# Adaptive-LayerNorm attention block: the early transfers as 128-row pieces, the first V tiles by column chunk, and group 1's V tiles in step

## The chip, the core and the metric

The kernel runs on one core of a Trainium2 chip. The core has five engines that the text calls by short names: PE (TensorE, matrix products, with PEld for its weight loads), DVE (VectorE), ACT (ScalarE), POOL (GpSimd) and SP (SyncE, which here only issues transfers). Sixteen DMA engines move data between HBM and the on-chip memory. The metric is the device time of one execution in microseconds, lower is better.

## The reference, cut to what matters

The input x has 2048 rows of 448 numbers. A vector c gives six modulation vectors of 448, three for the attention half (sa, ca, ga) and three for the other half.

```python
mod = (silu(c) @ w_mod).reshape(1, 6, 1, 448)          # c: 448, w_mod: 448 x 2688
sa, ca, ga, sb, cb, gb = (mod[:, i] for i in range(6))
h = layernorm(x) * (1 + ca) + sa
q, k, v = split(h @ wqkv)                              # wqkv: 448 x 1344, 16 heads of 28
x = x + ga * (softmax(q @ k.T * 28 ** -0.5) @ v) @ wo
h = layernorm(x) * (1 + cb) + sb
x = x + gb * gmlp(h, w_in, w_sp, b_sp, w_out)
```

Everything is float32. The change lies in the first part: mod, h, and the products of h with wqkv.

## The kernel before, in words

**Operands in two parts.** The operands of these products have the format fp32r. Each is written as the sum of a rounded part ("hi", an ACT activation that copies float32 into the format) and the rest ("lo", a subtraction, `sub`, L83). The 448 input columns are cut in chunks c = 0, 1, 2 of 128 and c = 3 of 64. hT[g] holds, for group g of 512 rows of x, slots 0 to 2 (hi of the chunks), 3 to 5 (lo) and 6 (hi and lo of the 64-row chunk, one above the other). A weight tile has the same slots and a slot 7. One product is the sum over the 11 pairs of slots in STEPS (L27 to L29), so 11 matmuls into one PSUM bank.

**Units of work.** A V tile (`v_mm`, L301) is 11 matmuls for 128 rows of x, and `v_copy` (L308, ACT) takes it out of PSUM. A q/k unit (`qk_unit`, L317) is 11 matmuls with 512 columns for one block m of 128 outputs and one group; ACT rounds the result (qh, L336) and DVE subtracts (ql). `ln_next` (L537) makes hT of a group: PE transposes the normalised rows (xn) into four banks (L117), ACT makes `hfull` (L124) and hi (L131) of each chunk, DVE the lo part, and in between the statistics of the group after it; POOL computes the scale (L107, L108), DVE the normalised rows (`ln_norm`, L286), and ACT copies their last 64 columns (L298).

**Order.** The order of each engine is the order in which the program text issues its instructions (manual schedule); nothing is moved. What one engine must wait for on another is set by the tiles: who writes a buffer waits for the last reader of what lay there before.

**PSUM.** There are eight banks. Seven form a ring: `bank` (L167) takes the first of the list `banks` and puts it at the end, so a new tile waits for the readers of the tile seven requests ago. The eighth, ps_o (L144), is asked for by name.

```python
    def bank(name):
        k = mode[0](name) if mode[0] else banks[0]
        banks.remove(k)
        banks.append(k)
        return ring.tile([128, 512], F32, name=name, tag=f"b{k}")
```

**The head.** x of group 0 comes in three pieces, the first two from ACT's queue (L181). The modulation weights of the pair (sa, ca) come in four pieces of 112 rows (`load_mod`, L176), V's weights in three pieces of 128 rows and two of 64, the same 64 rows put in both halves (`load_z`, L86), then x of group 1 and the "a" columns (0 to 511) of the q/k weights. silu(c) is made on ACT and DVE. The product with w_mod is a weighted sum on DVE over the four pieces (`acc`, L241) and then, chunk by chunk, `mod_last` (L407) and a dot with ones on PE (`mod_dot`, L420), which puts the sum of the partitions in one PSUM column; `mod_cols` (L423) takes it out. Then `h_hi` (L440), `h_full` (L431, on DVE) and `h_lo` (L445) make hT[0]. Between these steps PE runs matmuls whose result nobody reads (`pe_fill`, L228). The four V tiles of group 0 run in step (`v_step`, L474): the pair of slots is the outer loop, the tile the inner.

**After the head.** `qk_unit((0, 3), 0)` with both units in step (L530), `ln_next(1)` (L550), x of group 3, units 1 and 2 of group 0, the "b" columns of the q/k weights (L555). For group 1 the loop at L557 does V tiles 4 and 5, `ln_next(2)`, V tiles 6 and 7, then units 0 and 3, with one piece of the next modulation pair on DVE (`mod_acc`, L234) after each of the last four. Groups 2 and 3 follow the same way, then attention and the second half, to which the edits of `wo_load`, `win_first` and `win_load` belong.

Of the kernel before, what the change touches and what calls it, by code (L numbers as in the profile page):

```python
# [33 lines left out]
def tile_adaln_mha_gmlp(ctx, tc, x, wqkv, wo, w_in, w_spT, b_sp, w_out, cT, w_mod, out):  # L34
# [21 lines left out]
    silu = const.tile([112, 4], F32, name="silu")  # L56
# [6 lines left out]
    heapF = dpool.tile([128, 4 * 896], F32R, name="heapF", tag="heapF")  # L63
# [17 lines left out]
    wqk = Halves(4, hview(heapD[2], 0, 4, 896), hview(heapF, 0, 4, 896))  # L81

    def sub(eng, dst, a, hi):  # L83
        eng.tensor_tensor(out=dst, in0=a, in1=hi.bitcast(F32), op=ALU.subtract)  # L84

    def load_z(eng, dst, src):  # L86
        eng.dma_start(dst[0:64], src)
        eng.dma_start(dst[64:128], src)
# [71 lines left out]
    ones_r = e2.tile([112, 128], F32R, name="ones_r")  # L160
# [12 lines left out]
    def load_mod(pair, eng):  # L173
        for k in range(4):
            wms[pair, k] = e1.tile([112, 2, D], F32, name="wm", tag=("wm", "wm", "raw")[pair], bufs=4)
            eng.dma_start(wms[pair, k], w_mod[:, pair, k])  # L176

    def load_x(g, eng):
        xg = e1.tile([128, 4, D], F32, name="xg")
        for t0, t1 in ((0, 1), (1, 2), (2, 4)) if g == 0 else ((0, 4),):  # L180
            (act if t1 - t0 == 1 else eng).dma_start(xg[:, t0:t1, :], x[g, :, t0:t1])  # L181
        for t in range(4):
            xts[4 * g + t] = xg[:, t, :]
# [4 lines left out]
    def load_w(kind, i, eng):  # L188
        c0, n, tag = PARTS[kind]
        raw = e1.tile([128, 2 * D], F32, name="raw", tag=tag, bufs=4)[:, :n]  # L190
        if i < 3:
            eng.dma_start(raw, wqkv[i * 128 : (i + 1) * 128, c0 : c0 + n])
        else:
            load_z(eng, raw, wqkv[384:448, c0 : c0 + n])
        raws[kind, i] = raw
# [11 lines left out]
    cc_t = e1.tile([112, 4], F32, name="cc_t", bufs=1)  # L207
    sp.dma_start(cc_t, cT)
    load_x(0, sp)
    load_mod(0, sp)  # L210
    for i in (0, 2, 1, 3):
# [3 lines left out]
    pool.memset(wqk[64:128, 7, 0:896].bitcast(F32), 0.0)  # L215
# [3 lines left out]
    ec = e1.tile([112, 4], F32, name="ec", bufs=1)  # L219
    act.activation(ec, cc_t, AF.Exp, scale=-1.0)  # L220
    dve.tensor_scalar(out=ec, in0=ec, scalar1=1.0, scalar2=None, op0=ALU.add)
    dve.reciprocal(ec, ec)
    dve.tensor_tensor(out=silu, in0=cc_t, in1=ec, op=ALU.mult)

    pcs = {c: bank("pc") for c in (0, 2)}
# [8 lines left out]
    def mod_acc(pair, k):  # L234
        if k == 0:
            accs[pair] = e2.tile([112, 2, D], F32, name="acc")
        wm, acc = wms.pop((pair, k)), accs[pair]
        if k == 0:
            dve.tensor_scalar(out=acc, in0=wm, scalar1=silu[:, 0:1], scalar2=None, op0=ALU.mult)
        else:  # L240
            dve.scalar_tensor_tensor(out=acc, in0=wm, scalar=silu[:, k : k + 1], in1=acc, op0=ALU.mult, op1=ALU.add)  # L241

    def mod_split(pair, eng, pool_l, tag_l, bufs_l):
# [3 lines left out]
        for part in range(2):  # L247
            h = stage.tile([128, 512], F32R, name="acc_h", tag="qf")[0:112, :D]
            l = pool_l.tile([112, D], F32R, name="acc_l", tag=tag_l, bufs=bufs_l)
# [50 lines left out]

    def v_mm(kt):  # L301
# [12 lines left out]

    HI_FIRST = [p for p in STEPS if p[1] in (0, 1, 2, 6)] + [p for p in STEPS if p[1] in (3, 4, 5, 7)]
# [33 lines left out]
    def wv_hi(i):  # L349
        h = wv[:, i if i < 3 else 6, :]  # L350
        if i == 2:
            pool.tensor_copy(h, raws["v", i])
        else:
            act.activation(h, raws["v", i], AF.Copy)
# [8 lines left out]


    tps, fs = {}, {}
# [3 lines left out]
    def tp_first(t):  # L369
        for c in range(4):  # L370
            pe.transpose(tps[c][:, t * 128 : (t + 1) * 128], xn1[0][t][:, c * 128 : (c + 1) * 128], ident)

    x0, x3 = xts[0], xts[3]
    pe_fill(14, x0)
    ln_stat(0, (0, 1))
    ln_rs(0, 0, 2)
    ln_stat(0, (2, 3))
    ln_rs(0, 2, 4)
    accs[0] = e2.tile([112, 2, D], F32, name="acc")
    act.activation(accs[0], wms.pop((0, 0)), AF.Copy, scale=silu[:, 0:1])  # L380
    ln_norm(0, (0, 1))
    mod_acc(0, 1)
    tp_first(0)
    tp_first(1)
    ln_norm(0, (2, 3))
    mod_acc(0, 2)
    pe_fill(5, x3)
    tp_first(2)
    tp_first(3)
    pe_fill(2, x3)  # L390

    acc0 = [stage.tile([128, 512], F32, name="acc0", tag="qh")[0:112] for _ in range(2)]
    wm3 = wms.pop((0, 3))

    def mod_last(c):
        for part in (1, 0):
            if c < 3:
                o = acc0[part][:, c * 128 : (c + 1) * 128]  # L400
                a, w = (v[:, part, c * 128 : (c + 1) * 128] for v in (accs[0], wm3))
            else:
                o = acc0[part][:, 384:512].rearrange("p (r n) -> p r n", n=64)
                a, w = (
                    v[:, part, 384:D].rearrange("p (r n) -> p r n", r=1).broadcast_to([112, 2, 64]) for v in (accs[0], wm3)
                )
            dve.scalar_tensor_tensor(out=o, in0=w, scalar=silu[:, 3:4], in1=a, op0=ALU.mult, op1=ALU.add)  # L407

    def mod_dot(c, which):
        if c == 1:  # L410
            pcs[c] = ps_o.tile([128, 512], F32, name="pc", tag="o")
        if c == 3:
            pcs[c] = pcs[1][:, 2:4]
# [1073 lines left out]
```

## Time and profile before

| what | value |
|---|---|
| three executions | 1396.37, 1396.84, 1398.13 us (median 1396.84) |
| the profiled execution: its span, first to last instruction | 1394.0 us |
| what lies around the span, against the median | 2.84 us |
| PE busy | 1386.8 us of it |
| DVE, ACT, POOL busy | 1027.5, 776.5, 285.5 us |

The profile is one execution, and times in it count from its first instruction. The span is that execution's own time as the profile has it; no other time was taken of it. A row of the timeline gives the start, the time that the engine was busy, the engine, the line of the code, the operation, what it writes and reads, and how many instructions were merged in the row (x4); square brackets tell how long the engine stood idle before and who ended that. Rows of groups give busy time and the mean duration in ns, then the idle time before them. A row by stretch gives for each engine the busy time and the number of instructions, then the granted clock of PE (1.00 is full), the busy share of the DMA engines and the GB/s that they moved. Matmuls overlap, so the duration of one is longer than its distance to the next. Where two lines share a helper, the tile names tell them apart: L84 is every `sub`.

### The profile page before, as it was taken

How to read it: one execution, taken by the hardware profiler on the slowest of the kernel's cores; microseconds unless marked ns; L12 is line 12 of the kernel's file. 1: busy time of each engine (PE TensorE's matmuls, PEld its weight loads, DVE VectorE, ACT ScalarE, POOL GpSimd, SP SyncE). 2: the span in 40 equal slices, each digit the busy share in tenths (PEclk: the TensorE clock that was granted, in tenths of full speed). 3: DMA queues.
4: the chain of work that ended last, by engine and by line, in shares of the span. 5: the costliest groups of instructions: out<-in, count | busy, mean ns of one | idle time of the engine just before them, and what ended most of it. 6: DMA issues, size and time to landing. Idle time of an engine off the chain costs nothing.

```text
span 1394.0 us, 20327 instructions
## 1 busy us (share of the span) xinstructions
PE 1386.8 (99%) x7180; PEld 988.9 (71%) x7180; DVE 1027.5 (74%) x1741; ACT 776.5 (56%) x1490; POOL 285.5 (20%) x306
## 2 busy tenths in 40 slices
PE   8999999999999999999999999999999999999999
PEld 8888655555555555555555555988998888888888
DVE  7798888888888888888888851750366655668574
ACT  4623677777766667777777779363234544434211
POOL 2234213221224143323200021000142330000000
PEclk9999999999999999999999999999999999999999
DMA  8564644565465556554323002434103333445453
GB/s 265 150 178 177 196 109 151 172 177 154 149 178 167 162 159 189 165 161 150 111 68 76 21 18 73 161 123 140 46 4 110 113 109 112 143 137 163 142 174 110
DMA packets 99377, 187.01 MB, mean 134 GB/s; under 512 B 17736, under 2 KB 29130, under 8 KB 96730
## 3 DMA queue, kind: packets, MB, share of 16 engines
q1 hardware_dynamic: 96558, 181.42, 42.6%
q10 hardware_dynamic: 2718, 4.30, 0.9%
q8 instruction: 56, 0.92, 0.3%
q14 instruction: 45, 0.37, 0.1%
HBM read 130.42 MB, written 50.46 MB: 130 GB/s over the span
## 4 chain that ended last, share of the span: by engine, by line
PE 99%; DMA 0%; DVE 0%; ACT 0%; ACTq 0%; issue 0%
PE st_ps L666 19%; PE o_ps L681 17%; PE mt L634 17%; PE acc L1250 7%; PE acc L1252 7%; PE acc L1251 7%; PE z_ps L1176 5%; PE pq L323 5%; PE z_ps L1062 5%; PE wo_ps L928 3%; PE pv L305 2%; PE y_ps L1357 2%; PE y_ps L1358 2%; PE y_ps L1356 2%; PE tp L117 1%; PE pv L477 1%
## 5 line engine op out<-in xcount | busy, mean ns | idle before, releaser
L639 DVE TENSOR_REDUCE pm<-mt 128x1 f32<-128x512 f32 x1024 | 631.1, 682 | 85.6 <-PE mt L634 85.5
L670 ACT ACTIVATE P<-st_ps 128x512 f32<-128x512 f32 x1024 | 514.5, 628 | 200.8 <-PE st_ps L666 200.7
L666 PE MATMUL st_ps<-qst,kst 128*128 128x512 f32 x1024 | 404.1, 406 | 0.0
L634 PE MATMUL mt<-kst,qst 128*128 128x512 f32 x1024 | 401.7, 392 | 0.0
L666 PEld LDWEIGHTS st_ps<-qst,kst 128*128 128x128 f32 x1024 | 191.2, 187 | 141.2 <-issue 93.1
L681 PE MATMUL o_ps<-P,V 128*32 128x512 f32 x2048 | 247.1, 598 | 0.0
L634 PEld LDWEIGHTS mt<-kst,qst 128*128 128x128 f32 x1024 | 192.4, 188 | 31.8
L791 POOL TENSOR_TENSOR ws_raw<-ws_raw 128x512 f32<-128x512 f32 x80 | 103.2, 1290 | 293.8 <-DMA ws_raw<-in_w_spT_dram 290.9
L1138 ACT ACTIVATE wsp_h<-raw_sp 128x512 fp32r<-128x512 f32 x112 | 70.0, 630 | 153.6 <-PE acc L1252 102.9
L84 DVE TENSOR_TENSOR wsp_l<-raw_sp,wsp_h 128x512 fp32r<-128x512 f32 x112 | 80.7, 730 | 83.1 <-ACT wsp_h L1138 82.3
L681 PEld LDWEIGHTS o_ps<-P,V 128*32 128x32 f32 x2048 | 54.7, 109 | 122.0 <-issue 114.0
L1250 PE MATMUL acc<-wsp_h,heapA 128*128 128x512 f32 x224 | 87.3, 390 | 0.0
L1251 PE MATMUL acc<-wsp_l,heapA 128*128 128x512 f32 x224 | 87.2, 389 | 0.0
L1252 PE MATMUL acc<-wsp_h,heapA 128*128 128x512 f32 x224 | 87.2, 389 | 0.0
L1251 PE MATMUL acc<-wsp_l,heapB 128*128 128x512 f32 x174 | 67.7, 389 | 0.0
L1252 PE MATMUL acc<-wsp_h,heapB 128*128 128x512 f32 x174 | 67.7, 389 | 0.0
L1250 PE MATMUL acc<-wsp_h,heapB 128*128 128x512 f32 x174 | 67.7, 389 | 0.0
L323 PE MATMUL pq<-heapD,heapD 128*128 128x512 f32 x196 | 61.8, 390 | 0.0
L1180 DVE BATCH_NORM_STATS2 stz<-z 128x6 f32<-128x448 f32 x32 | 19.9, 625 | 50.4 <-ACT z L1179 30.1
L1250 PEld LDWEIGHTS acc<-wsp_h,heapA 128*128 128x128 f32 x224 | 42.0, 188 | 8.9 <-DVE cD L1256 0.3
L1252 PEld LDWEIGHTS acc<-wsp_h,heapA 128*128 128x128 f32 x224 | 42.0, 188 | 8.8
L1251 PEld LDWEIGHTS acc<-wsp_l,heapA 128*128 128x128 f32 x224 | 42.0, 188 | 8.6
(222 smaller groups left out, 1597.0 us busy)
## 6 DMA issues: line engine op xcount, KB each, us to landing
ws_raw<-in_w_spT_dram SPq DMA_DIRECT2D x160, 256.0 KB
ws_scr<-ws_raw SPq DMA_DIRECT2D x80, 256.0 KB
raw_sp<-ws_scr SPq DMA_DIRECT2D x80, 256.0 KB
kst<-qk_scr SPq DMA_DIRECT2D x45, 224.0 KB
qst<-qk_scr SPq DMA_DIRECT2D x45, 224.0 KB
raw_sp<-in_w_spT_dram SPq DMA_DIRECT2D x32, 256.0 KB
qk_scr<-qh SPq DMA_DIRECT2D x28, 256.0 KB
qk_scr<-ql SPq DMA_DIRECT2D x28, 256.0 KB
```

Source lines behind the costliest of these rows:

```text
L84: eng.tensor_tensor(out=dst, in0=a, in1=hi.bitcast(F32), op=ALU.subtract)
L323: pe.matmul(pq, wqk[:, b, m * 128 : (m + 1) * 128], hT[g][:, a, :], start=j == 0, stop=j == NST - 1)
L634: pe.matmul(mt, qst[h % 3][:, t * 128 : (t + 1) * 128], kst[h % 3][:, kb * 512 : (kb + 1) * 512], start=True, stop=True)
L639: dve.tensor_reduce(out=pms[h][:, t, kb : kb + 1], in_=mt, axis=AX.X, op=ALU.max)
L666: pe.matmul(st, kst[h % 3][:, kt * 128 : (kt + 1) * 128], qst[h % 3][:, qb * 512 : (qb + 1) * 512], start=True, stop=True)
L670: act.activation(p, st, AF.Exp, scale=SCALE)
L681: pe.matmul(otile[h][32 * qb : 32 * qb + 32, :], V[:, kt, h, :], ptiles.pop((u, qb)), start=kt == 0, stop=kt == NT - 1)
L791: pool.tensor_tensor(out=a, in0=a, in1=b, op=SUMS[i // 16][2])
L1138: act.activation(hi, raw, AF.Copy)
L1250: pe.matmul(acc[i], zh, hi, start=st == 0, stop=False)
L1251: pe.matmul(acc[i], zh, lo, start=False, stop=False)
L1252: pe.matmul(acc[i], zl, hi, start=False, stop=st == 7)
```

## The change

**Transfers.** The host repeats the last 64 rows of wqkv, wo and w_in, so that the fourth piece of each weight is one transfer of 128 rows; `load_z` is gone. w_mod of the first pair is laid out by column chunk: piece c has 128 rows, each with the chunk's columns for three blocks of 128 inputs and both vectors, and the last 64 inputs of the one vector above those of the other. The pairs 1 and 2 keep their four steps, now with 128 rows, the last one folded in the same way. silu becomes a 128x5 tile, whose last two columns are zero in one half. The first pair lies in the buffer of the upper q/k weight slots (heapF), which is taken for them only after the head. All of x goes through SP, c through ACT; chunks and V weights alternate in the order 0, 2, 3, 1; the "a" loads are issued after the head's work instead of in its midst.

**Head.** Chunk 0 of the modulation is eight matmuls on PE (`mod_direct`); the other chunks start with a product on ACT (`acc_first`), go on with four weighted sums on DVE (`acc_rest`) and end with the dot with ones. PE fills once, 10 pairs of instructions, instead of 27 in five places. `h_full` goes from DVE to ACT, the lo part of chunk 0 from POOL to DVE, the hi part of V's weights 2 from POOL to ACT. The V steps run chunk by chunk.

**Behind the head.** Unit 1 of group 0 goes ahead of `ln_next(1)`. Group 1's four V tiles run in step, in three banks of the ring and ps_o, with `ln_next(2)` called after the ninth step; their copies and the first two `mod_acc` follow the loop.

The core of the diff (edits of sizes from 112 to 128, the repeated rows and removed definitions are left out):

```diff
+    wm0 = dpool.tile([128, 4 * 896], F32, name="wm0", tag="heapF")
...
+    def load_mod0(c, eng):
+        n = 128 if c < 3 else 64
+        v = wm0[:, c * 896 : c * 896 + 7 * n]
+        eng.dma_start(v, w_mod0[c * 896 * 128 : (c * 896 + 7 * n) * 128].rearrange("(r n) -> r n", r=128))
+        wms[0, c] = v[:, 0 : 6 * n].rearrange("r (k p n) -> r k p n", k=3, p=2), v[:, 6 * n :]
...
-        if i < 3:
-            eng.dma_start(raw, wqkv[i * 128 : (i + 1) * 128, c0 : c0 + n])
-        else:
-            load_z(eng, raw, wqkv[384:448, c0 : c0 + n])
+        eng.dma_start(raw, wqkv[i * 128 : (i + 1) * 128, c0 : c0 + n])
...
-    sp.dma_start(cc_t, cT)
+    act.dma_start(cc_t, cT)
     load_x(0, sp)
-    load_mod(0, sp)
-    for i in (0, 2, 1, 3):
+    for i in (0, 2, 3, 1):
+        load_mod0(i, sp)
         load_w("v", i, sp)
     load_x(1, sp)
...
+    def half_rows(wm, outs):
+        for part, o in enumerate(outs):
+            dve.scalar_tensor_tensor(out=o, in0=wm, scalar=silu[:, 3 + part : 4 + part], in1=o, op0=ALU.mult, op1=ALU.add)
...
+    CHUNKS = [(0, 0), (0, 3), (3, 0), (2, 2), (2, 5), (5, 2), (1, 1), (1, 4), (4, 1), (6, 6), (6, 7)]
...
+    def mod_direct(c):
+        wm, wh = wms.pop((0, c))
         for i, part in enumerate((1, 0)):
+            for k in range(3):
+                pe.matmul(pc_of(c, i), wm[:, k, part, :], silu[:, k : k + 1], start=k == 0, stop=False)
+            pe.matmul(pc_of(c, i), wh, silu[:, 3 + part : 4 + part], start=False, stop=True)
+
+    def acc_first(c):
...
+        act.activation(o, wms[0, c][0][:, 0], AF.Copy, scale=silu[:, 0:1])
+
+    def acc_rest(c):
+        (wm, wh), o = wms.pop((0, c)), acc0[c]
+        for k in (1, 2):
+            dve.scalar_tensor_tensor(out=o, in0=wm[:, k], scalar=silu[:, k : k + 1], in1=o, op0=ALU.mult, op1=ALU.add)
+        half_rows(wh, [o[:, part] for part in range(2)])
...
+    x0 = xts[0]
+    pe_fill(10, x0)
+    ln_norm(0, (0, 1))
     wv_hi(0)
+    mod_direct(0)
+    for t in (0, 1):
+        for c in range(4):
+            tp_first(c, (t,))
+    acc_first(2)
+    ln_norm(0, (2, 3))
+    for c in (0, 2, 1, 3):
+        tp_first(c, (2, 3))
     mod_cols(0)
+    acc_rest(2)
     h_hi(0)
+    h_full(0)
     wv_lo(0, dve)
...
+    order = [(0, 0), (0, 3), (3, 0), (2, 2), (2, 5), (5, 2), (6, 6), (6, 7), (1, 1), (1, 4), (4, 1)]
+    pvs = [(kt, bank("pv")) for kt in range(2)]
+    pvs.append((2, ps_o.tile([128, 512], F32, name="pv", tag="o")))
...
     v_step(0, (0, 1, 2))
+    mod_dot(2)
+    mod_cols(2)
+    h_lo(0, dve)
+    wv_hi(2)
+    h_hi(2)
+    acc_first(3)
+    h_full(2)
+    v_step(1, (0, 1, 2))
+    v_step(2, (0, 1, 2))
+    wv_lo(2, dve)
+    acc_rest(3)
+    acc_first(1)
+    h_lo(2, dve)
+    mode[0] = lambda name: tp0_bank
+    pvs.append((3, bank("pv")))
+    mode[0] = None
+    for j in range(3):
+        v_step(j, (3,))
+    v_step(3, range(4))
+    mod_dot(3)
+    mod_cols(3)
+    wv_hi(3)
+    h_hi(3)
+    h_full(3)
+    acc_rest(1)
+    h_lo(3, dve)
+    wv_lo(3, dve)
+    v_step(4, range(4))
+    v_step(5, range(4))
+    mod_dot(1)
+    wv_hi(1)
+    mod_cols(1)
     h_hi(1)
+    h_full(1)
     wv_lo(1, dve)
     h_lo(1, dve)
+    for i in (0, 2, 1, 3):
+        load_w("a", i, sp)
     load_x(2, sp)
...
     qk_unit((0, 3), 0, order=HI_FIRST)
+    qk_unit((1,), 0)
...
     ln_next(1)
     load_x(3, sp)
-    qk_unit((1,), 0)
     qk_unit((2,), 0)
...
+        if g == 1:
+            pvs = [(kt, bank("pv") if kt < 7 else ps_o.tile([128, 512], F32, name="pv", tag="o")) for kt in range(4, 8)]
+            for j, (a, b) in enumerate(CHUNKS):
+                for kt, pv in pvs:
+                    pe.matmul(
+                        pv[:, :D], hT[1][:, a, (kt - 4) * 128 : (kt - 3) * 128], wv[:, b, :], start=j == 0, stop=j == NST - 1
+                    )
+                if j == 8:
+                    ln_next(2)
+            for kt, pv in pvs:
+                v_copy(kt, pv)
+            mod_acc(1, 0)
+            mod_acc(1, 1)
+            for k, m in enumerate((0, 3)):
+                qk_unit((m,), 1)
+                mod_acc(1, 2 + k)
+            continue
```

## What the change was predicted to do

> **What bounds the kernel now.** I read the page first, then the busy time by stretches, then the chain that ended last in order of time.
>
> ```profile
> span 1394.0 us, 20327 instructions
> ...
> PE 1386.8 (99%) x7180; PEld 988.9 (71%) x7180; DVE 1027.5 (74%) x1741; ACT 776.5 (56%) x1490; POOL 285.5 (20%) x306
> ```
> ```profile
> core 0: us, PE busy (x) PEld busy (x) DVE busy (x) ACT busy (x) POOL busy (x), PEclk, DMA share, GB/s
> 3.00:4.50 1.50, 0.89 (x4) 0.92 (x5) 1.02 (x4) 0.21 (x1) 0.61 (x1) 1.00 1.02 388
> 7.50:10.50 3.00, 2.93 (x27) 2.70 (x26) 2.51 (x6) 1.33 (x3) 1.42 (x3) 1.00 1.03 279
> 15.00:18.00 3.00, 2.93 (x20) 2.67 (x19) 2.86 (x10) 2.15 (x5) 0.31 (x1) 1.00 1.00 385
> 14.87:84.00 69.13, 69.06 (x354) 61.48 (x353) 57.90 (x100) 40.25 (x79) 16.16 (x17) 1.00 0.67 192
> 84.00:1390.50 1306.50, 1306.50 (x6749) 916.56 (x6747) 959.61 (x1614) 731.23 (x1402) 263.72 (x276) 1.00 0.42 130
> 1393.00:1394.00 1.00, 0.00 (x0) 0.00 (x0) 0.00 (x0) 0.00 (x0) 0.00 (x0) 0.50 0.00 0
> ```
> ```profile
> 17.22 8.02 PE pv L477 x38
> 25.24 5.02 PE pq L323 x22
> ...
> 37.01 4.48 PE pv L305 x22
> 43.23 4.49 PE pv L305 x22
> ```
>
> From 14.87 us to 1390.50 PE is busy for 1375.56 of 1375.63 us. So the change can win only ahead of 14.9, where PE mostly runs filler, and every stall it makes behind that point is added to the end whole. The chain gives what PE costs per matmul: 4.48 / 22 = 0.204 us for V, 5.02 / 22 = 0.228 for a q/k unit (a unit of 11 is 2.5).
>
> **The first part: the transfers and V of group 0.**
>
> ```profile
> 5.72 0.63 DVE L279 BATCH_NORM_STATS2 st<-xg 128x6 f32<-128x448 f32 x1 [0.92 <-DMA xg<-in_x_dram]
> ...
> 8.59 0.82 POOL L108 TENSOR_TENSOR rs<-rs,mhalf 128x2 f32<-128x2 f32 x1
> ...
> 12.67 0.58 PE L420 MATMUL pc<-ones,acc 112*128 112x1 f32 x4
> ...
> 14.90 0.85 PE L477 MATMUL pv<-wv,heapD 128*128 128x448 f32 x3
> ```
> ```profile
> L436 DVE TENSOR_SCALAR hfull<-tp,col_ca,col_sa 128x512 f32<-128x512 f32 x4 | 3.1, 804 | 0.0
> L241 DVE SCALAR_TENSOR_TENSOR acc<-wm,silu,acc 112x896 f32<-112x896 f32 x2 | 2.3, 1150 | 0.5 <-DMA wm<-in_w_mod_dram 0.5
> L84 DVE TENSOR_TENSOR wv<-raw,wv 128x448 fp32r<-128x448 f32 x3 | 1.9, 617 | 0.0
> ...
> L407 DVE SCALAR_TENSOR_TENSOR acc<-wm,silu,acc 112x128 f32<-112x128 f32 x6 | 1.7, 345 | 0.0
> L84 DVE TENSOR_TENSOR heapD<-hfull,heapD 128x512 fp32r<-128x512 f32 x2 | 1.3, 688 | 0.0
> ```
> ```profile
> L441 ACT ACTIVATE heapD<-tp,col_sa,col_ca 128x512 fp32r<-128x512 f32 x4 | 3.1, 778 | 1.7 <-DVE col_sa L429 0.8 <-DVE col_sa L427 0.8
> L354 ACT ACTIVATE wv<-raw 128x448 fp32r<-128x448 f32 x3 | 1.7, 570 | 0.7 <-DMA raw<-in_wqkv_dram 0.7
> ```
>
> The stretch at 7.5 holds 112-row w_mod pieces and moves 279 GB/s; those at 3.0 and 15.0 hold 128-row x pieces and move 388 and 385. With 128 rows throughout I take 385. [...] x (0.92 MB, 2.4 us) has passed near 4.8, and DVE's wait for it ends at 5.72, so I add 1 us to each landing. Behind x come 0.46 (w_mod chunk 0), 0.23 (V weights 0), 0.46, 0.23, 0.23, 0.23, 0.46 and 0.23 MB, 1.19 us per 0.46 MB: landings at 7.0, 7.6, 8.8, 9.4, 10.0, 10.6, 11.7, 12.3.
>
> x's pieces now follow each other on SP, where today two stand on ACT's queue beside the rest, so I let its statistics end 0.9 earlier (estimate); POOL's second scales, at 8.59 + 0.82 = 9.4 today, then come at 8.5. PE: 20 fill instructions to 7.5; mod_direct, 16 instructions of 0.11 (four of today's dots take 0.58 with the last one's tail), to 9.3; 16 transposes to 11.1. h_hi(0) runs on ACT from 10.7 to 11.5, so the first V step is at 11.6 against 14.90: **3.2 us earlier**. A 256-wide weighted add I put at 0.40, between 0.28 (128 wide: 1.7 / 6) and 1.15 (896 wide), near the first.
>
> From there DVE, one queue in written order, paces. Its list, with ends: norms 9.5; columns 0 9.8; acc_rest(2) (2 x 0.40, 2 x 0.28) 11.1; wv_lo(0) 11.7; it then waits for mod_dot(2), behind the first V step on PE, and ends columns 2 at 13.2; h_lo(0) 13.8; wv_lo(2) 14.35; acc_rest(3) 15.4; h_lo(2) 16.05; it waits for mod_dot(3) and ends columns 3 at 17.25; acc_rest(1) 18.65; h_lo(3), held by ACT's h_full(3) until 18.85, 19.55; wv_lo(3) 20.1; columns 1 20.4; wv_lo(1) 20.95; then ACT's h_hi(1) and h_full(1) (0.78 each) to 22.0, and h_lo(1) to **22.75**. h_full, 0.804 on DVE today, sits on ACT, h_lo(0) comes from POOL to DVE and wv_hi(2) from POOL to ACT; they are in the list. The last V matmuls follow h_lo(1): V ends on PE at 23.8 against 25.1. The head wins 1.3 us, not 3.2. Were DVE never to hold PE, it would win 3.2 less 0.9 (16 dot instructions stand inside V, 8 today), 2.3.
>
> **The second part: group 1's V in step.** I count the ring of seven banks (L165 to L171) through the new code. wu takes 0, transposes 1 to 4, V tiles 0 and 1 take 5 and 6, tile 2 the eighth bank, tile 3 bank 1; units 0 and 3 of group 0 take 0 and 2, unit 1 takes 3; group 1's transposes 4, 5, 6, 1; unit 2 takes 0; V tiles 4, 5, 6 take 2, 3, 4 and tile 7 the eighth; group 2's transposes 5, 6, 1, 0. Next is unit 0 of group 1: **bank 2, tile 4's**. It has to wait for tile 4's copy. That copy stands on ACT behind everything that ln_next(2) puts there, the xn copies of group 3 included, for ln_next(2) is called at the ninth of the 11 steps and the copies follow the loop. Today tiles 6 and 7 stand there:
>
> ```profile
> 41.00 1.07 ACT L336 ACTIVATE qh<-pq 128x512 fp32r<-128x512 f32 x2
> ...
> 44.46 0.79 ACT L124 ACTIVATE hfull<-tp,col_sa,col_ca 128x512 f32<-128x512 f32 x1
> ...
> 49.28 0.63 ACT L131 ACTIVATE heapD<-hfull 128x512 fp32r<-128x512 f32 x1
> ...
> 52.23 0.83 POOL L108 TENSOR_TENSOR rs<-rs,mhalf 128x2 f32<-128x2 f32 x1
> ...
> 53.10 0.94 DVE L290 TENSOR_SCALAR xn<-xg,mv,rs 128x448 f32<-128x448 f32 x2 [0.61 <-POOL rs L108]
> ...
> 54.07 0.26 ACT L298 ACTIVATE xn<-xn 128x64 f32<-128x64 f32 x1 [0.16 <-DVE xn L290]
> 54.23 0.96 ACT L309 ACTIVATE V<-pv 128x448 f32<-128x448 f32 x2
> ```
> ```profile
> 47.56 0.86 PE L323 MATMUL pq<-heapD,heapD 128*128 128x512 f32 x3
> ```
>
> Tiles 6 and 7 are done on PE by 47.7, and their copies start at 54.23; nobody waits today, for the next units get other banks. From ACT's first hfull at 44.46 to the end of the first copy (54.23 and half of 0.96) are 10.3 us: 8 activations, then DVE's last split and statistics, POOL's scales, DVE's norms, the xn copies. I carry this over.
>
> When does that hfull start? Today:
>
> ```profile
> 22.93 0.61 DVE L279 BATCH_NORM_STATS2 st<-xg 128x6 f32<-128x448 f32 x1
> 28.26 1.77 DVE L290 TENSOR_SCALAR xn<-xg,mv,rs 128x448 f32<-128x448 f32 x4
> 31.24 0.78 ACT L124 ACTIVATE hfull<-tp,col_sa,col_ca 128x512 f32<-128x512 f32 x1
> 40.83 0.26 ACT L298 ACTIVATE xn<-xn 128x64 f32<-128x64 f32 x1 [0.17 <-DVE xn L290]
> ```
>
> After h_lo(1) at 22.75 DVE has two splits of "a" weights (0.6 each), so the statistics of group 1 start at 24.0, not 22.93, and its norms end near 30.9, not 30.03. ACT then has three q/k roundings (1.07 / 2 each) ahead of group 1's hfull, unit 1 having moved ahead of ln_next(1), where two stand today: 32.7, not 31.24. The xn copies of group 2 end as long after it as today, 9.85 us, at 42.55, not 41.09. From there to group 2's hfull are 3.37 us today; one rounding (0.53) and two V copies (0.96) fewer leave 1.9: hfull at **44.45**, first copy done at **54.75**.
>
> PE meanwhile: V 23.8, three units 31.3, transposes 33.1, unit 2 35.6, group 1's V (44 x 0.204) with 16 transposes (1.8) 46.4. Then it idles until 54.85, 8.4 us, and starts unit 0 of group 1 **7.3 us later** than at today's 47.56. All of PE's later work is queued behind the waiting matmul. The 1.3 us of the head only lengthen the idle time.
>
> **The clock.**
>
> ```profile
> L230 PE MATMUL wu<-ones,xg 128*128 128x128 f32 x15 | 3.5, 430 | 3.6 <-DMA xg<-in_x_dram 3.6
> ```
> ```profile
> L230 PE MATMUL wu<-ones,xg 128*128 128x128 f32 x13 | 1.7, 285 | 0.0
> ```
> ```profile
> 1390.15 0.37 PE L1358 MATMUL y_ps<-heapB,uT 128*128 128x448 f32 x1
> ```
>
> The last matmul ends at 1390.52, and the granted clock is 0.50 in the stretch at 1393: less than 3 idle us take the clock away. The fills between 3.9 and 6.8 take 430 ns, those between 7.3 and 8.4 285 ns: full speed comes some 3.5 us after the first matmul. 8.4 idle us thus cost the clock, and the units run at half speed for about 3.5 us: **+1.7** (0 if it held, 3.2 if the release took twice as long).
>
> **The other edits, at nothing.** "a" loads, now behind x 1 on SP, land near 17 and are wanted at 22; POOL's clearing of wqk moves behind the last reader of w_mod's buffer, near 19, and is wanted at 28; mod_acc's half rows are two adds for one on DVE, and its move behind the V copies delays nothing that PE wants soon. Single transfers for wo and w_in lie in the stretch from 84, where PE has no idle time to give back. Uncovered, each is under 1 us.
>
> **Sum.** 7.3 + 1.7 = 9.0 us on the span of 1394.0. The median of 1396.84 stands 2.84 above it, and I keep that: 1396.84 + 9.0 = **1405.8**. My hand-made queues may be off by 1.5 either way and the clock costs 0 to 3.2: 1402.6 to 1408.9.
>
> **Rivals.**
>
> *The copy is no obstacle* (not slower). If tile 4's copy ended by 46.4, where PE asks for bank 2, the head's gain stays: 1.3 to 2.3 us, 1395.5 to 1394.5, within 0.2%. It decides at that point: the copy's end against the end of group 1's V. Against it: the row at 54.23, where ACT keeps its written order for 6.5 us. 8%. A head that wins over 2.8 us besides: 3%.
>
> *The clock falls in the head too.* The new head has 10 fills and then only dots of one column and transposes until 11.6. If PE then has half the clock, the 12 V matmuls up to mod_dot(3) take 2.0 us more, DVE's columns 3 and the whole line behind them slip as much: 1407.8. For it: the later fills are gone; against it: today's PE keeps its speed through 8 transposes at a time. 9%. [...]
>
> *The 128-row transfers bring nothing.* At 279 GB/s V weights 1 land 2.5 us later, near 14.8, still ahead of their use at 18.8; the first chunks slip by 1 at most, and the line behind them with it: 1406.8, since the wait swallows the head anyway. Inside the forecast's range and chance.
>
> **Chances.** 80% for the forecast, 9% for 1407.8: slower 0.89; within 0.2% (2.8 us, about what a measurement of this kernel can tell from no change) 0.08; faster 0.03. The range of 1402.6 to 1408.9 covers the forecast and most of the second rival; it leaves out the first rival and some mishaps.
>
> **What the changed profile would show.** The first V matmul near 11.6 and some 385 GB/s until 14; V of group 0 ending near 24; PE idle for 8 to 9 us between 46 and 55 ahead of a unit of L323's kind, released by ACT's copy into V; a clock of 0.50 in that gap and slow matmuls for 3 to 4 us behind it; no idle time later. No such gap refutes me; a gap with the clock kept makes it 1404.1.

## The result, and the profile after

The changed kernel took **1410.34 us** (median of four runs, 1409.52 to 1411.43) beside 1397.38 for the kernel before (1396.37 to 1398.13): ratio 1.0094, 95% interval 1.008 to 1.0108, so 13.0 us slower. Forecast was 1405.8, at most 1408.9. The profiled spans differ by 15.6 us (1409.6 against 1394.0). A span is some 1.8 us shorter than the time of its own execution (1409.6 beside 1411.43 for after's), so before's profiled execution was about 1.6 us quicker than its median and after's, the slowest of its four, 1.1 us slower. That makes up the difference between 15.6 and 13.0.

The wait that was foretold is there. First PE's timeline of the changed kernel around it, then ACT's:

```profile
48.92 1.89 PE L584 MATMUL pv<-wv,heapD 128*128 128x448 f32 x8
59.59 1.65 PE L333 MATMUL pq<-heapD,heapD 128*128 128x512 f32 x3 [8.78 <-ACT V L318]
...
67.05 1.18 PE L314 MATMUL pv<-wv,heapD 128*128 128x448 f32 x5
```
```profile
33.85 1.07 ACT L346 ACTIVATE qh<-pq 128x512 fp32r<-128x512 f32 x2
36.93 0.60 ACT L346 ACTIVATE qh<-pq 128x512 fp32r<-128x512 f32 x1 [2.01 <-DMA qk_scr<-qh]
37.42 0.77 ACT L118 ACTIVATE hfull<-tp,col_sa,col_ca 128x512 f32<-128x512 f32 x1
...
49.28 0.77 ACT L118 ACTIVATE hfull<-tp,col_sa,col_ca 128x512 f32<-128x512 f32 x1
...
58.85 0.26 ACT L298 ACTIVATE xn<-xn 128x64 f32<-128x64 f32 x1 [0.17 <-DVE xn L290]
59.01 1.82 ACT L318 ACTIVATE V<-pv 128x448 f32<-128x448 f32 x4
```

The last V matmuls of group 1 end at 50.8; the first copy stands at 59.01, behind the last xn copy of group 3, and unit 0 starts when the first quarter of the 1.82 is over. PE is idle for 8.78 us. The wait is hardly longer than the forecast 8.4, but only because PE came late as well (50.8, forecast 46.4): unit 0 starts 12.0 us later than before (47.56), not 7.3. The row at 36.93 has a wait that the prediction does not hold: the third rounding stands 2.01 us for a transfer, the store of the first one, which has to leave its buffer. The 22 matmuls up to 67.05 take 7.46 us, against 5.02 before: the clock.

The busy time by stretches (after the times: PE, PEld, DVE, ACT, POOL, then granted clock, DMA share, GB/s), and PE's and DVE's timelines of the head:

```profile
3.00:6.00 3.00, 2.44 (x11) 2.47 (x12) 1.92 (x7) 0.21 (x1) 0.80 (x2) 1.00 0.88 252
...
9.00:10.50 1.50, 1.50 (x14) 1.50 (x13) 0.98 (x3) 0.75 (x3) 1.17 (x2) 0.84 1.05 403
10.50:12.00 1.50, 1.50 (x9) 1.50 (x10) 1.42 (x5) 1.14 (x4) 0.05 (x1) 0.50 1.06 410
...
10.10:16.70 6.60, 6.60 (x30) 6.47 (x30) 3.23 (x11) 3.45 (x8) 0.45 (x1) 0.50 1.04 407
...
54.50:64.50 10.00, 4.91 (x12) 3.90 (x13) 5.32 (x11) 2.95 (x9) 1.69 (x3) 0.50 0.18 73
```
```profile
8.80 0.80 PE L385 MATMUL wu<-silu,wm 128*128 128x1 f32 x6 [1.32 <-DMA wm<-in_w_mod_dram]
...
11.11 3.65 PE L376 MATMUL tp<-ident,xn 128*128 128x128 f32 x16
14.41 1.47 PE L452 MATMUL pv<-wv,heapD 128*128 128x448 f32 x3
```
```profile
7.58 0.63 DVE L279 BATCH_NORM_STATS2 st<-xg 128x6 f32<-128x448 f32 x1 [2.08 <-DMA xg<-in_x_dram]
...
24.92 0.69 DVE L82 TENSOR_TENSOR heapD<-hfull,heapD 128x512 fp32r<-128x512 f32 x1 [0.98 <-ACT hfull L414]
```

128-row pieces move 403 to 410 GB/s once the stream runs, but the stretch from 3 to 6 only 252, where before had 388 in its first half and 336 in its second. x's last piece comes at 7.58 (before 5.72), chunk 0 of w_mod at 8.7 (forecast 7.0). From 10.1 to 16.7 the clock is 0.50 and the 16 transposes take 3.65 us. The first V step is at 14.41 (forecast 11.6, before 14.90), h_lo(1) ends at 24.92 + 0.69 = 25.61 (forecast 22.75).

### The profile page after: what moved, and what is told of

Its sections match the earlier page's. It is cut to its first block, busy times and chain, and to the rows that moved or that the text cites. A ratio compares the mean times of both kernels' runs of the same rounds, so it can differ in the third digit from the quotient of the medians.

```text
span 1409.6 us, 20280 instructions
## 1 busy us (share of the span) xinstructions
PE 1391.7 (99%) x7158; PEld 990.3 (70%) x7158; DVE 1026.7 (73%) x1744; ACT 779.9 (55%) x1497; POOL 281.1 (20%) x304
## 4 chain that ended last, share of the span: by engine, by line
PE 96%; DVE 1%; DMA 1%; ACT 0%; POOL 0%; issue 0%; SPq 0%; DVEq 0%; ACTq 0%; POOLq 0%
PE st_ps L675 18%; PE o_ps L690 17%; PE mt L643 17%; PE acc L1250 6%; PE acc L1251 6%; PE acc L1252 6%; PE z_ps L1176 5%; PE z_ps L1062 5%; PE pq L333 4%; PE wo_ps L931 3%; PE y_ps L1357 2%; PE y_ps L1358 2%; PE y_ps L1356 2%; PE pv L314 1%; DMA wm<-in_w_mod_dram 1%; PE tp L111 1%
## 5 line engine op out<-in xcount | busy, mean ns | idle before, releaser
L333 PEld LDWEIGHTS pq<-heapD,heapD 128*128 128x128 f32 x196 | 37.8, 194 | 16.9 <-ACT V L318 9.2
```

Source lines behind the costliest of these rows:

```text
L333: pe.matmul(pq, wqk[:, b, m * 128 : (m + 1) * 128], hT[g][:, a, :], start=j == 0, stop=j == NST - 1)
```

## The experiments

My theory after this: the wait for tile 4's bank is the main part, made longer by a late head and by the store wait, and the clock adds its price. Rivals: the head or unit 1's new place alone make most of it; or the bank is beside the point, and ACT's late order would be waited for anyway. "Over before" is (ratio - 1) x 1397 us.

| run | what it is | median us | ratio, 95% interval | over before |
|---|---|---|---|---|
| after | the change | 1410.34 | 1.0094 (1.008 to 1.0108) | 13.1 |
| 1 | before, and group 1's V in step | 1407.31 | 1.0067 (1.0053 to 1.008) | 9.4 |
| 2 | after, V copies ahead of ln_next(2) | 1401.69 | 1.0031 (1.0019 to 1.0042) | 4.3 |
| 3 | the head alone | 1400.66 | 1.0025 (1.0017 to 1.0034) | 3.5 |
| 4 | after, unit 1 back | 1408.82 | 1.0077 (1.0062 to 1.0093) | 10.8 |
| 5 | 3, third place for the rounding | 1398.31 | 1.001 (1.0002 to 1.0019) | 1.4 |
| 6 | 3, more filler | 1403.18 | 1.0042 (1.0029 to 1.0056) | 5.9 |
| 7 | 3, x on two queues | 1399.14 | 1.0021 (1.0013 to 1.003) | 2.9 |
| 8 | after, filler in the wait | 1415.49 | 1.0131 (1.0117 to 1.0145) | 18.3 |
| 9 | after, other banks | 1399.34 | 1.0022 (1.0013 to 1.0031) | 3.1 |
| 10 | 9 with 5 and 7 | 1396.72 | 1.0002 (0.9993 to 1.001) | 0.3 |
| 11 | 3 with 5 and 7 | 1397.14 | 1.0008 (0.9999 to 1.0017) | 1.1 |
| 12 | 11, transposes as filler | 1401.15 (one run) | | |
| 13 | 11, dots as filler | 1415.79 (one run) | | |
| 14 | 10, one more turn of the ring | 1396.29 | 0.9992 (0.9983 to 1.0001) | -1.1 |

### 1, 2, 3: the two halves of the change

Run 1 puts only the in-step loop for group 1 into the kernel before.

```diff
+        if g == 1:
...
+            pvs = [(kt, bank("pv") if kt < 7 else ps_o.tile([128, 512], F32, name="pv", tag="o")) for kt in range(4, 8)]
+            for j, (a, b) in enumerate(chunks):
+                for kt, pv in pvs:
+                    pe.matmul(...)
+                if j == 8:
+                    ln_next(2)
+            for kt, pv in pvs:
+                v_copy(kt, pv)
...
```

> The kernel before with one edit: group 1's V tiles in step as in the changed kernel; head, transfers and all else are the old ones. Theory W (bank wait): the old ring gives unit 0 of group 1 the bank of tile 4 as well, and tile 4's copy stands on ACT behind ln_next(2). In the trace of before that place is reached at 54.2; two copies fewer ahead make it about 53.5 to 54. PE idles 6 to 6.5 us ahead of that unit, loses its clock, and the time is 8 to 9 us above before: 1405 to 1406.5. Rival H (the new head's lateness makes the gap): on the old head the step order costs nothing, 1397 to 1398.

Its timelines of PE and of ACT, and its busy time by stretches:

```profile
54.80 1.65 PE L323 MATMUL pq<-heapD,heapD 128*128 128x512 f32 x3 [7.44 <-ACT V L309]
```
```profile
44.48 0.78 ACT L124 ACTIVATE hfull<-tp,col_sa,col_ca 128x512 f32<-128x512 f32 x1 [1.13 <-PE tp L117]
...
54.23 1.83 ACT L309 ACTIVATE V<-pv 128x448 f32<-128x448 f32 x4
```
```profile
50.90:60.90 10.00, 6.09 (x14) 4.81 (x15) 4.60 (x9) 3.36 (x9) 1.24 (x2) 0.50 0.04 11
```

Unit 0 waits for the copy of V and starts 7.24 later than before's 47.56, with an untouched head: the forecast's 7.3. The clock falls too (0.50 from 50.9 to 60.9). 9.4 us: the step alone is worth most of the loss. Both the wait (6 to 6.5 expected) and the time (1405 to 1406.5) came out larger than expected, because the two V copies that no longer stand on ACT win nothing: group 2's transposes now stand behind nine steps of V on PE, and ACT waits 1.13 us for them. The copies start at 54.23, as in before. The forecast came to nearly the same place by other terms (a later list on DVE, one rounding more, two copies fewer), so that 7.24 and 7.3 agree is in part luck.

Run 2 takes the obstacle away by order.

```diff
-                if j == 8:
-                    ln_next(2)
             for kt, pv in pvs:
                 v_copy(kt, pv)
+            ln_next(2)
```

> The changed kernel with ln_next(2) called after the four V copies of group 1, so that the copies stand ahead of it on ACT. Theory W: the idle 8.8 us and the half clock behind it (2.4 us) go, hT of group 2 is late by at most 1: 1398.5 to 1400.5, some 11 us under the changed kernel and 1 to 3 above before, since the head is late. Rival H: the late head is what costs; the gap only moves to the V tile behind and the time stays over 1405.

The wait is gone (unit 0 at 48.4), with 4.3 us left, a little over the 1 to 3 that were expected: PE waits for DVE instead, 0.40 us for a lo part of group 2's h (at 55.9) and 1.18 and 1.00 us for banks whose q/k result DVE has not split yet (61.5 and 63.2). Run 3 keeps only the head, with unit 1 in its new place: the changed kernel with before's loop for group 1.

```diff
-        if g == 1:
-            pvs = [...]
...
-            continue
```

> The changed kernel with group 1's V tiles one after the other as before (ln_next(2) after two of them); transfers and head are the new ones. Theory W: no bank is asked for early, so no gap of 8 us; but the head ended 1.6 us later on PE than before and hT of group 1 was ready 2 us after PE wanted it, tile by tile PE waits for each chunk: 1400 to 1403. My prediction's step (the head wins 1.3): 1396. Rival H: near 1410.

3.5 us slower, where the prediction had the head win 1.3. 9.4 + 3.5 = 12.9: the two halves add up to the 13.1 of the whole. PE's timeline of run 3 shows where it goes, ACT's and the stretches what is wrong in the head:

```profile
36.84 0.47 PE L314 MATMUL pv<-wv,heapD 128*128 128x448 f32 x1
38.17 2.53 PE L314 MATMUL pv<-wv,heapD 128*128 128x448 f32 x8 [0.86 <-ACT heapD L125]
41.70 2.92 PE L314 MATMUL pv<-wv,heapD 128*128 128x448 f32 x13 [1.00 <-DVE heapD L82]
...
46.46 4.75 PE L314 MATMUL pv<-wv,heapD 128*128 128x448 f32 x22
```
```profile
34.86 0.60 ACT L346 ACTIVATE qh<-pq 128x512 fp32r<-128x512 f32 x1 [2.01 <-DMA qk_scr<-qh]
```
```profile
3.60:6.00 2.40, 2.40 (x12) 2.40 (x13) 1.59 (x7) 0.08 (x1) 0.95 (x2) 1.00 0.80 252
8.00:11.30 3.30, 2.94 (x27) 2.94 (x28) 2.66 (x9) 1.85 (x6) 1.22 (x2) 1.00 1.03 395
11.40:14.70 3.30, 3.30 (x15) 3.12 (x14) 2.04 (x8) 1.92 (x3) 0.00 (x0) 0.50 1.03 412
```

PE reaches group 1's V at 36.84, as in before, but the third tile only at 46.46 (before 42.99): it waits for the parts of group 1's h, which ACT begins at 35.35 instead of 31.24. Three suspects make them late: the store wait (2.01 again), the slow start of the transfers (252 GB/s again), the clock (0.50 from 11.4 to 14.7).

### 4 and 5: the store wait

Run 4 moves `qk_unit((1,), 0)` back behind `ln_next(1)`.

```diff
 qk_unit((0, 3), 0, order=HI_FIRST)
-qk_unit((1,), 0)
...
 load_x(3, sp)
+qk_unit((1,), 0)
 qk_unit((2,), 0)
```

> The changed kernel with unit 1 of group 0 back behind ln_next(1). Theory: the third rounding on ACT waited 2.0 us for the store of the first (two buffers), and that wait lies in the line that ends in tile 4's copy; without it hfull of group 1, and so the copy and the end of the gap, come 2 to 2.5 us earlier: 1407.5 to 1408.5. If that wait is hidden: 1410 to 1411.

ACT's timeline of run 4:

```profile
48.65 0.78 ACT L118 ACTIVATE hfull<-tp,col_sa,col_ca 128x512 f32<-128x512 f32 x1 [0.92 <-PE tp L111]
...
58.40 1.83 ACT L318 ACTIVATE V<-pv 128x448 f32<-128x448 f32 x4
```

The time fell by 1.5, between the two expectations. The store wait is gone: group 1's hfull stands at 35.28 instead of 37.42, in a profile whose first V step came 0.97 later. But ahead of group 2's hfull ACT now waits 0.92 us for PE's transposes, so the copies start only 0.61 earlier (58.40 against 59.01). This run can't price the store wait by itself. Run 5 leaves the order of run 3 alone and gives the rounding a place that is free:

```diff
+            if ms == (1,) and g == 0:
+                hi, lo = hT[3][:, 0, :], hT[3][:, 1, :]
+            else:
                 hi = stage.tile([128, 512], F32R, name="qh")
                 lo = stage2.tile([128, 512], F32R, name="ql")
```

> The head alone, with unit 1 of group 0 writing its two rounded parts to a place of its own (two planes of group 3's h, empty until then), so that its rounding need not wait for a store. Theory (the store wait is a term of the loss): the 2.0 us by which that rounding stood goes, the two idle stretches of PE at 38.2 (0.86) and 41.7 (1.0) go with it, and the time falls from 1400.7 to some 1398.8 (1398.0 to 1399.5). Rival (the wait is covered; DVE's later list and the late first V step hold group 1's h anyway): 1400.0 to 1401.2, and PE stays idle at 38 to 42.

ACT's and PE's timelines of run 5:

```profile
33.05 0.60 ACT L349 ACTIVATE heapD<-pq 128x512 fp32r<-128x512 f32 x1
33.53 0.79 ACT L118 ACTIVATE hfull<-tp,col_sa,col_ca 128x512 f32<-128x512 f32 x1
```
```profile
39.91 2.91 PE L314 MATMUL pv<-wv,heapD 128*128 128x448 f32 x13 [1.00 <-DVE heapD L82]
```

No bracket at 33.05: the rounding follows at once. The time falls by 2.35 by the medians and by 2.1 by the ratios, as the theory had it. Of PE's two idle stretches in run 3 the 0.86 goes, the 1.00 stays, where both were expected to go; it is for the last lo part of group 1's h.

### 6 and 7: the head's clock and its transfers

Run 6 adds filler to run 3, run 7 goes back to two queues for x (and to SP for c).

```diff
             pe.matmul(pc_of(c, i), wh, silu[:, 3 + part : 4 + part], start=False, stop=True)
+            pe_fill(4, x0)
...
-    pe_fill(10, x0)
+    pe_fill(17, x0)
...
+    pe_fill(4, ident)
     acc_first(2)
```

> The head alone, with 7 more fill matmuls ahead of the first dots, 4 behind each set of 8 dots' halves (8 in all) and 4 between the two sets of transposes. Theory (PE's clock falls because dots of one column and transposes do not keep it): no record of 0.50 between 8 and 17 us; the V matmuls take 0.2 instead of 0.37 us each from the first on; the 12 fills on the path cost 1.3 of the 2.3 us won: 1399.2 to 1400.2. Rival (the clock falls whatever stands there, for instance so many us after the start): the record of 0.50 stays, and the fills cost 1.3 to 2.5: 1402 to 1403.

I had miscounted: a filler call is two instructions, so the 19 additional calls made 38 instructions. The clock did stay up (8 transposes in 1.04 us, the first three V matmuls in 0.88 against 1.48 in run 3), but the first V step slid to 16.19, 3.9 later than in run 3, and the run lost 2.5 against it instead of winning 0.5 to 1.5. It shows that the fall can be prevented, not that it pays. Run 7:

```diff
-            eng.dma_start(xg[:, t0:t1, :], x[g, :, t0:t1])
+            (act if t1 - t0 == 1 else eng).dma_start(xg[:, t0:t1, :], x[g, :, t0:t1])
...
-    act.dma_start(cc_t, cT)
+    sp.dma_start(cc_t, cT)
```

> The head alone, with the first two pieces of x on ACT's queue again and c on SP's, as before. Theory (one queue for all of x is why 3.6 to 6.0 us moved only 252 GB/s where before moved 388 in 3.0 to 4.5): that rate is back above 350, x's statistics end near 6.4 instead of 8.2, the first dots start near 7.5 instead of 8.4, the first V step near 11.4 instead of 12.3, time 1399.5 to 1400.2. Rival (the rate is that of the mixed pieces, whatever their queue): first dots at 8.3 to 8.7, 1400.4 to 1401.2.

The stretches and PE's timeline of run 7:

```profile
3.60:6.00 2.40, 2.40 (x11) 2.40 (x12) 1.22 (x3) 0.00 (x0) 0.00 (x0) 1.00 1.03 398
7.80:11.10 3.30, 3.30 (x31) 3.15 (x31) 2.66 (x9) 1.94 (x7) 1.22 (x2) 1.00 1.07 410
11.20:14.60 3.40, 2.99 (x18) 2.28 (x17) 3.03 (x9) 2.92 (x6) 0.00 (x0) 1.00 1.00 396
```
```profile
9.59 2.08 PE L376 MATMUL tp<-ident,xn 128*128 128x128 f32 x16
11.88 0.87 PE L452 MATMUL pv<-wv,heapD 128*128 128x448 f32 x3 [0.21 <-ACT heapD L417]
```

398 GB/s in place of 252, nothing idle ahead of the dots, the clock held, 16 transposes in 2.08 instead of 3.65. The first V step at 11.88 and the end of group 0's V at 23.6 are what was forecast (11.6 and 23.8). In time that is 1.5 by the medians but 0.6 by the ratios, whose intervals overlap. Why one queue is slower over its first pieces (its share of the engines, the order of issue, or c's move in the same edit) was not taken apart.

### 8 and 9: the wait itself

Run 8 fills the wait with 76 calls of filler, to hold the clock.

```diff
+            mode[0] = lambda name: banks[3]
+            wu2 = bank("wu2")
+            mode[0] = None
+            for _ in range(76):
+                pe.matmul(wu2[:, 0:128], ident, ident, start=True, stop=True)
```

> The changed kernel with 76 matmuls of 128 columns (8.4 us at full speed) put into the wait ahead of unit 0 of group 1, written to a bank whose readers are done by then; they compute nothing that is used. Theory (the idle wait also costs the clock, worth 2.4 us): the wait for the copy stays, no record of 0.50 between 54 and 65 us, and the time falls from 1410.3 to 1407.9 (1407.2 to 1408.6). Rival (the clock's fall costs nothing that the next wait would not have cost): 1409.8 to 1410.8. If the fills run beyond the copy's end they add what they overrun, under 1 us.

PE's timeline of run 8:

```profile
50.69 17.13 PE L597 MATMUL wu<-ident 128*128 128x128 f32 x152
67.58 0.94 PE L333 MATMUL pq<-heapD,heapD 128*128 128x512 f32 x3
```

The same miscount: 152 instructions, and unit 0 starts at 67.58, 8.0 later than in after. But the run is only 5.15 longer. The difference, 2.8 us, is what the kept clock gives back (its units run at full speed: 0.94 for three matmuls, against 1.65). The rows alone give 2.35: the 22 matmuls take 5.11 here (67.58 to 72.69) and 7.46 in after. The rest is less than the medians can tell.

Run 9 leaves ACT's order and gives unit 0 the bank of a transpose:

```diff
             mod_acc(1, 1)
+            banks[:] = banks[3:] + banks[:3]
             for k, m in enumerate((0, 3)):
```

> The changed kernel with the ring's list turned by three places ahead of units 0 and 3 of group 1, so that unit 0 gets the bank of a transpose (read by 50.1) and not that of V tile 4; ACT's order, the copies behind ln_next(2), stays. Theory (it is the bank, and only through it the copy): units 0 and 3 start at 50.9 instead of 59.6, the copies still end at 59.5 to 60.8 and hold nobody, the wait shrinks from 8.8 to under 1 us and the clock stays: 1400.8 (1399.8 to 1402.2), what remains being the head's. Rival (whatever stands behind ACT's late order is waited for anyway, as the q/k rounding behind the copies): 1404 to 1409.

PE's and ACT's timelines of run 9:

```profile
48.53 0.86 PE L333 MATMUL pq<-heapD,heapD 128*128 128x512 f32 x3
```
```profile
56.90 1.83 ACT L318 ACTIVATE V<-pv 128x448 f32<-128x448 f32 x4
```

The copies are as late as ever in ACT's order (56.9), and nobody waits for them: unit 0 starts 8.4 us ahead of them. One line, 10 us. It is the bank, and the late copy only through it. Unit 0 came before the 50.9 that was expected, and the time just under its range, since in this profile the first V step stood at 13.15 and not at 14.41.

### 10, 11, 14: all repairs

Run 10 is run 9 with the edits of 5 and 7, run 11 the head alone with those two.

> The changed kernel with the ring turned as in the run beside it, unit 1's roundings in a place of their own, and x's first two pieces on ACT's queue. If the three terms add: 1400.8 less 2.35 less 1.5, 1397.0 (1396.0 to 1398.5), as long as before. Rival (what one repair frees the next wait takes, since DVE's list after the first V step sets group 1's h): 1399 to 1401.

> The head alone (group 1's V as before), with unit 1's roundings in a place of their own and x's first two pieces on ACT's queue. If the two terms add: 1400.7 less 2.35 less 1.5, 1396.8 (1396.0 to 1397.8), against 1397.0 for the kernel before: the 128-row transfers then bring nothing that lasts, though V of group 0 ends 1.6 earlier. Rival (they bring the 1.3 that was predicted for the head): 1395.5 to 1396.

The terms add: both are level with before. The head's V ends at 23.56 in run 10, 1.68 earlier than before, yet attention starts only 0.5 earlier. PE's timeline of run 10 shows where most of that goes:

```profile
58.22 2.09 PE L314 MATMUL pv<-wv,heapD 128*128 128x448 f32 x9 [0.90 <-DVE ql L82]
```

V tile 10 asks for the bank of unit 3, which DVE has not finished rounding. Run 14 turns the ring by one place more ahead of that tile.

```diff
+        if g == 2:
+            banks.append(banks.pop(0))
         for k in range(2):
             v_tile(4 * g + 2 + k)
```

> The kernel with all three repairs, and the ring turned by one more place ahead of V tile 10, so that it gets V tile 8's bank (copied at 56.7) and not that of unit 3, whose second rounding DVE ends at 58.16. Theory (of the 1.67 us that the head wins, this wait of 0.90 is what eats the larger part): the wait goes, attention starts 1.4 earlier than in before instead of 0.5, 1395.9 (1395.2 to 1396.6). Rival (the next wait takes it): 1396.4 to 1397.2.

PE's timeline of run 14 has no bracket there:

```profile
57.05 4.74 PE L314 MATMUL pv<-wv,heapD 128*128 128x448 f32 x22
...
62.78 0.47 PE L258 MATMUL pc<-acc_l,ones_r 128*128 128x448 f32 x1 [0.39 <-POOL acc_l L82]
```

Attention starts 1.0 earlier than before, not the expected 1.4: 0.39 of it goes into a new wait for POOL at 62.78. The time is 1396.29, the ratio 0.9992 (0.9983 to 1.0001): the best version of the study, and not to be told from the kernel before.

### 12 and 13: what holds the clock

Run 7 keeps its clock over dots and transposes (16 dots from 7.88 to 9.59, 16 transposes in 2.08 us); runs 2, 3 and 5, with 0.4 to 0.5 us idle ahead of the dots, lose it. This is not the chance of one profile: 7, 10 and 14, with x on two queues and this filler, all keep it there (1.00 from 10.1 to 16.7, with 41 to 43 PE instructions in it, where after has 0.50 and 30); of the seven with x on one queue five (after, 2, 3, 5, 9) are at 0.50 by 12.0, and the other two (4, 8) have not got it yet (16 transposes in 3.65 us). Two kernels replace the matmul of the filler of run 11 by one of the two lines below, and `pe_fill(10, x0)` by `pe_fill(48, x0)`.

```diff
-            pe.matmul(wu[:, 0:128], with_[:, 0:128], ones, start=True, stop=True)
+            pe.transpose(wu[:, 0:128], with_[:, 0:128], ident)        # run 12
+            pe.matmul(wu[:, 0:1], with_[:, 0:128], ones[:, 0:1], start=True, stop=True)        # run 13
```

> The repaired head, whose filler ahead of the dots (20 matmul records of 128 columns) is replaced by 48 transposes, which leave nothing that is used. Theory (transposes keep and raise the clock like matmuls; the dots of one column are what lost it): the clock goes to 1.00 within two steps of 3.41 us of the first, by 10.5 us at the latest, the later transposes pass every 0.11 us and the first V step comes near 15. Rival (transposes count for nothing): 0.21 us for every transpose and dot up to the first V step, which comes near 21, and the clock rises only behind it.

> The same with 48 dots of one column in place of the filler. Theory (dots count for little): 0.21 us for every dot, no record of 1.00 ahead of the transposes at 17 us, first V step at 19 to 21. Rival (any dense row of PE instructions counts, and idle time alone lost the clock): 1.00 by 10.5 us, first V step near 15.

PE's timeline of run 12, then of run 13, where each of the 48 calls is two instructions (a transpose is one):

```profile
3.51 8.06 PE L222 MATMUL wu<-ident,xg 128*128 128x128 f32 x48 [3.51 <-DMA xg<-in_x_dram]
...
15.27 0.88 PE L455 MATMUL pv<-wv,heapD 128*128 128x448 f32 x3 [0.21 <-ACT heapD L420]
```
```profile
3.46 20.61 PE L222 MATMUL wu<-ones,xg 128*128 128x1 f32 x96 [3.46 <-DMA xg<-in_x_dram]
```

48 transposes take 8.06 us: 0.21 each at first (17 in the 3.50 us from 3.5), then about half that (16 in the 1.50 us from 9.0, where run 13 has 9 dots). The 96 dots take 20.61, 0.215 each to the end, without one idle moment, so the first V step can't stand at the expected 19 to 21: the same miscount. **Here 48 transposes alone brought full speed within 8.06 us; 96 dots of one column alone had not brought it in 20.61.** How the dots' step looks in the stretches of run 13 is worth a second look:

```profile
17.50:21.00 3.50, 3.50 (x18) 3.50 (x18) 0.00 (x0) 0.00 (x0) 0.00 (x0) 1.00 0.02 5
```

The clock column says 1.00 at half speed (18 instructions in 3.50 us; run 12 has 34 in the 3.50 us from 10.5). It does so in after too, from 3.6 to 6.0, where 11 instructions take 2.40 us and the trace's first clock record stands only at 6.60: ahead of that record the column is no measurement, and the instructions' own pace tells the truth.

## Why the prediction was wrong

The time came out 4.5 us above the forecast and 1.4 above its range.

**Right: the mechanism.** The bank, the copy behind ln_next(2), the wait, the clock's fall, no idle time on PE behind it. That the wait has the forecast length (8.78 against 8.4) is luck: PE came 4.4 late and the copy 4.7. From group 1's hfull on, the carried spans held: 9.82 us to the end of group 2's xn copies (carried: 9.85; 46.98 + 0.26 - 37.42 in ACT's timeline), 2.0 to group 2's hfull (1.9), 10.2 to the end of the first copy (10.3). "The copy is no obstacle" (8%) fell with runs 1 and 9.

**Failed: "ACT then has three q/k roundings ahead of group 1's hfull: 32.7".** I moved an instruction and counted its 0.53 us, but not the buffer it writes. Two qh buffers serve three roundings in a row, and the third waits for the first one's store: 2.0 us of the 4.7 by which hfull was late (37.42 against 32.7), and 2.35 in run 5. The edit stood nowhere among those "at nothing" either.

**Failed: "x's pieces now follow each other on SP ... 0.9 earlier", and "landings at 7.0".** The rate of 385 GB/s was right and low for the middle of the stream (403 to 410). But it holds only from 7.5 us on (342 between 6.0 and 7.5): with all of x on one queue 3 to 6 us moved 252. x's last piece came 1.9 later than in before, where I had it 0.9 earlier, and chunk 0 came 1.7 later than forecast. The premise of "The 128-row transfers bring nothing", a rate that stays at 279, is refuted by the rows over 400, though in time even the repaired head wins nothing that can be told (run 11). That it is the 128 rows that make the rate is not shown: the row count was not changed alone, the layout of the pieces in memory changed with it.

**Failed: the clock in the head, the rival at 9%.** It came true: 0.50 from 10.0 to 16.8. Together with the late landings the first V step came 2.8 late (14.41 against 11.6). That size is this execution's: the seven profiles with this head have the step at 12.31 to 15.38 (the last section has what the clock did in them). From there DVE took 11.2 us to h_lo(1), forecast 11.15, and that is luck in part: with the clock kept (run 7) it took 10.3, so my list was 0.8 too long and the half clock made up for it. Of the two kinds of instruction that this rival names, runs 12 and 13 show half speed with the dots of one column (still 0.215 us each after 20.61 us of them), full speed with these float32 transposes (0.21 us each at first, then about half).

**Mis-sized: the clock's price in the gap**, 1.7 forecast, 2.4 by the matmuls of after (7.46 less 5.02), 3.0 by those of run 1 (8.03 from 54.80 to 62.83) and 2.8 by run 8's time. I took one row of 3.5 us for the return; it took 5.0 in after (59.59 to 64.6) and 6.2 in run 1 (54.80 to some 61.0). In after the clock stood at 0.50 for 10.24 us, from 54.39 to 64.63, and in run 1 for some 10.2 (an estimate from its clock of 0.54 from 50 to 60 us and 0.95 from 60 to 70): the matmuls had half speed for what was left of that when they began.

**Sum.** 7.3 + 2.0 + 2.8 = 12.1 for unit 0's delay, measured 12.0; with 2.4 of clock 14.5, as measured at the first V tile of group 2 (67.05 against 52.56). A last 1.0 us of the profile's 15.6 comes up behind the start of attention; what makes it stays open. The sum is that of the profiled execution; the medians are 13.0 apart. The range had 1.5 for errors of my lists, where the head and the store each cost more than that, and both on the same side, since any delay ahead of the copy delays unit 0 in full.

## What to carry to other kernels

Before a tile loop is widened, write down for each PSUM bank of the ring who reads it last and where that reader stands in its engine's order; a bank asked for early with a reader placed late is a stall that one turn of the list can remove (8.8 us here). When an instruction moves, count the buffers it writes as well as its time: the third writer in a row into two buffers waits for the slowest reader, here a store (2.0 us). Where filler is removed ahead of short instructions, ask what keeps PE's clock (96 dots of one column had not raised it here in 20.61 us), and look at the matmuls' own pace where the clock column has no record.

## What was not expected of the hardware

In after the clock's records stand at 6.60, 10.01, 16.84, 54.39 and 64.63: their distances are 1, 2, 11 and 3 times 3.41 us. The same head came to full speed at different times. In after the first record, of 1.00, stands at 6.60. In run 3 the last 5 of the filler still take 1.27 us from 6.72 (8 of run 6's take 1.14 later, at full speed), and the dots 0.11 apiece from 8.36. In runs 4 and 8 the 16 dots (from 8.67 and from 8.11) take 0.21 apiece and the 16 transposes 3.65 us; the first four dots at full speed (0.50, against 0.85 in after and in run 3) start at 16.49 and 16.03. What PE did between the records, its busy time there and the clock that followed:

| run | from one record to the next | in it | PE busy, us | clock in it | clock behind it |
|---|---|---|---|---|---|
| after | 6.60 to 10.01 | filler, 1.32 us idle, dots | 2.09 | 1.00 | 0.50 |
| after | 10.01 to 16.84 | dots, 16 transposes, V, 4 dots | 6.83 | 0.50 | 1.00 |
| after | 54.39 to 64.63 | 5.2 us idle, q/k matmuls | 5.04 | 0.50 | 1.00 |
| before | 7.17 to 1392.98 | PE's work until 1390.52, then idle | 1383.2 | 1.00 | 0.50 |

Dots of one column and transposes differ: dots and nothing else for 20.61 us left run 13 at half speed, where transposes alone brought run 12 to full speed within 8.06. How much work of which kind brings the clock or keeps it is not shown: PE was busy throughout for 6.83 us at half speed in after's head, and in its gap the clock came back behind 5.04 us.
